# Retention and a Mish feed-forward on one core: the last g sum moved behind the second pair, the sums of w_in for the last tile moved, and one block of the first product moved

## The chip, the cores and the metric

The kernel runs on one core of a Trainium2 chip. The metric is the time of one execution on the device in microseconds (us); the median of several executions counts. A second number beside it is the span, from the first to the last instruction of the program in a profiled execution.

## The reference

```
scores = (q @ k.T) / sqrt(64)                  # q, k, v: 8 batches, 8 heads, 576 rows, 64
ret    = (scores * gamma[h]**(i - j), 0 above the diagonal) @ v
x      = ret, heads side by side               # 4608 tokens x 512
h      = x @ w_in                              # 512 x 2048
g      = h * tanh(softplus(h))                 # Mish
out    = g @ w_out                             # 2048 x 512, float32
```

## The kernel before

**Tiles.** The 4608 tokens are cut into 36 chunks of 128, and four chunks make a tile: nine tiles, t = 0 to 8. While the first product (x @ w_in) of tile t runs, the second product (g @ w_out) of tile t-1 runs between its pieces, and the retention of the next tile's chunks as well, all of it on the same engines. The order on each engine is the order in which the code issues the instructions.

**The second product** uses seven products of half-size matrices in place of eight. Each of the seven is done in two halves, `unit(t-1, k)` for k = 0 to 13, called U0 to U13 below, in the order of products 4, 2, 1, 3, 6, 5, 7 (`ORDER`). Product 7 is thus U12 and U13. One U is eight matmuls at L659. Five of the seven need a sum of two quarters of g; `g_sum(t-1, m)`, called Sm below, makes it on VectorE (L650) in one of three buffers `room`. S7 is read by product 7 alone. When a product is complete, `taken` brings its bank to SBUF on ScalarE (L682, L684, L690, L697, L709) or adds it in on VectorE (L699, L712). L712 takes product 7 and so frees the bank `ops` for product 4 (U0) of the next tile.

**The first product.** `g1(t, f)`, called g4 to g15, makes one block of 128 columns of h: four matmuls (L571) into a bank `hp` of a pool of two, then Mish on ScalarE (L587). The first four columns of blocks in a tile are made by two pairs (A0 with B0, A1 with B1) with seven products in place of eight. `pair_begin` (A) does four small products (L810) into the banks `across` and `along`, ScalarE copies (L830, L831), and GpSimd adds (L832, L833). `pair_end` (B) does three small products more, VectorE combines (L844 reads `across`, L846 reads `along`), and ScalarE applies Mish (L845, L848). The sums of x that the pairs need come from `x_sums` (job X, L805), five on VectorE.

**The last tile** (t = 8, `last` and `tail`) does all its first product by pairs, seven of them. For them it needs sums of quarters of w_in over five more column blocks: `w_in_sum(m)` (L783), five on VectorE, made during t = 7.

**The order around the change.** `PLAN` is written out by hand: sixteen slots for a tile, each a list of jobs, used for t = 3 to 7. In a slot the S and X jobs are issued first, then what belongs to the retention, then the other jobs in order. From t = 3 to 6, slots 4, 5, 12 and 13 each end with the scaling of q and k of one chunk (`step_p`, two instructions at L352 on VectorE); later SyncE transposes it (L374). In slots 6 and 14 a retention visit (L386, L504 and others on TensorE, the mask L392 on VectorE, the copies L516 or L561 on ScalarE) stands ahead of the jobs; for some chunks (`WHOLE`) the slot's jobs are taken in reverse, U12 ahead of g14. GpSimd issues the loads of later chunks (L335, L339); each waits for the latest Mish of a `g1` issued before its slot (`load_ahead`, `so_far`).

The slot's loop, in short:

```
    for t in range(NS, nT - 1):
        for i in range(nF):
            ...
            if t == nT - 2 and i in W_IN:
                w_in_sum(W_IN[i])
            ...
            if t == nT - 2 and i == 15:
                rest()
                x_sums(nT - 1)
            ...
            for job in PLAN[i] ...:   # S and X jobs
            ...                       # retention
            for job in ...:           # A, B, g, U jobs
            ...                       # scaling of a chunk, loads
```

Of the kernel before, what the change touches and what calls it, by code (L numbers as in the profile page):

```python
# [16 lines left out]
def kernel(  # L17
# [40 lines left out]
    nT = n_chunks // NCH  # L58
# [415 lines left out]
    def run(jobs, *how):  # L474
        while jobs:
            jobs.pop()(*how)
# [41 lines left out]
    def visit(n, banks, copies, masked=True):  # L518


        units = states(n + 2)
        for unit in units[:1]:
            unit()
        both = [pool.tile([P, NP, 2, 64], F32, name=name) for pool, name in banks]
        outputs(n, both)
        seen = written(outputs_end(n, both, 0))
        if units:
            step_s(n + 2)
        for unit in units[1:]:
            unit()  # L530
        outputs_end(n, both, 1, seen)
        outputs_copy(n, both, copies)
        if units and masked:
            step_m(n + 2)
# [108 lines left out]
    def g_sum(t, i, engine=nc.vector, to=None):  # L643
        a, b, op_ = {1: ((0, 0), (1, 1), OP.add), 2: ((1, 0), (1, 1), OP.add), 5: ((0, 0), (0, 1), OP.add),
                     6: ((1, 0), (0, 0), OP.subtract), 7: ((1, 1), (0, 1), OP.subtract)}[i]
        if to is None:
            to = room[3 + gsum.setdefault("n", 1) % 3]
            gsum["n"] += 1
        to = to.rearrange("p (f i) -> p f i", f=hF)
        engine.tensor_tensor(to, g_half(t, *a), g_half(t, *b), op=op_)  # L650
        gsum[i] = to
# [18 lines left out]
    def rest():  # L670
        while behind_visit:
            behind_visit.pop(0)()
# [93 lines left out]
    def w_in_quarter(i, j, lo=0, hi=nS):  # L766
        return w_in_t[:, ds(hK * j, hK), :].rearrange("p c (b i q) -> p c b i q", i=2, q=P)[:, :, lo:hi, i, :]

    def w_in_sum_first(i):

        a, b, op_ = W7[i]
        to = {1: kept[:, 0], 5: kept[:, 1], 6: kept[:, 2]}.get(i)
        if to is None:
            to = w_in_quarter(*{2: (1, 0), 7: (0, 1)}[i])
        nc.vector.tensor_tensor(to, w_in_quarter(*a), w_in_quarter(*b), op=op_)
        w7[i, 0] = to

    def w_in_sum(i):

        a, b, op_ = W7[i]  # L780
        to = io.tile([P, 2, H, D], F32, name="qkraw").rearrange("p i h d -> p (i h d)").bitcast(BF16)
        w7[i, 1] = to[:, 0:hK * (nB - nS) * P].rearrange("p (c b q) -> p c b q", c=hK, q=P)
        nc.vector.tensor_tensor(w7[i, 1], w_in_quarter(*a, nS, nB), w_in_quarter(*b, nS, nB), op=op_)  # L783
# [9 lines left out]
    def x_sums(t):  # L793

        if not x_room:
            x_room.append(first.tile([P, 2, H, D], BF16, name="k0", bufs=2).rearrange("p x h d -> p (x h d)"))
            x_room.append(first.tile([P, 2, NP, 64], F32, name="s0", bufs=4)
                          .rearrange("p x n d -> p (x n d)").bitcast(BF16))
            x_room.append(consts.tile([P, hK * hT], BF16, name="xsum"))
        x = lambda j, k: xts[t][:, ds(hK * j, hK), ds(hT * k, hT)]  # L800
        for m, (i, a, b, op_) in enumerate(((3, (0, 1), (1, 1), OP.subtract), (4, (1, 0), (0, 0), OP.subtract),
                                            (6, (0, 0), (0, 1), OP.add), (1, (0, 0), (1, 1), OP.add),
                                            (7, (1, 0), (1, 1), OP.add))):
            x7[i] = x_room[m // 2][:, ts(m % 2, hK * hT)].rearrange("p (c k) -> p c k", c=hK)
            nc.vector.tensor_tensor(x7[i], x(*a), x(*b), op=op_)  # L805
        x7[5], x7[2] = x(1, 1), x(0, 0)
# [274 lines left out]
    for u in range(2, 24):  # L1081
# [43 lines left out]


    PLAN = [x.split() for x in (
        "X S2 g4 g5 U0|S1 U1|A0 U2|g6 U3 B0|g7 U4|U5|g8 U6|S6 g9|U7 g10|S5 U8 g11|U9|S7 A1|g12 U10 B1|g13 U11|g14 U12|g15 U13").split("|")]
    PACED = (1, 2, 3, 4, 5, 6)
    HALVED = {}  # L1130
    WHOLE = (16, 20, 22, 26, 28, 32)
# [14 lines left out]
                load_part(n, part)  # L1146

    LOADS = (2, 3, 4, 5, 6, 7, 8, 9, 11, 12, 13, 14)
    W_IN = {6: 1, 7: 2, 8: 6, 10: 5, 11: 7}
    W_IN_FIRST = {7: 1, 8: 5, 9: 6, 10: 2, 11: 7}  # L1150
    for t in range(NS, nT - 1):
        for i in range(nF):
            n, w = NCH * (t + 1) + i // 8 * 2, i % 8
            copies_first = i == 8 and n - 2 in WHOLE
            if w == (2 if t == NS else 0) and not copies_first:
                run(casts, act)
            if t == nT - 2 and i in W_IN:
                w_in_sum(W_IN[i])
            if t == NS and i in W_IN_FIRST:
                w_in_sum_first(W_IN_FIRST[i])  # L1160
            if t == nT - 2 and i == 15:
                rest()
                x_sums(nT - 1)
            if (t, i) in HALVED:
                halved[0] = HALVED[t, i]
            for job in PLAN[i] if t > NS else {5: ("S5",), 9: ("S7",)}.get(i, ()):
                if job[0] == "S":
                    g_sum(t - 1, int(job[1]))
                elif job == "X":
                    x_sums(t)  # L1170
            if t == NS:
                if w == 6:
                    visit(n, ((ps_h, "hp"), (ps_h, "hp")), (act, act))
            elif n in WHOLE:
                if w == 6:
                    visit(n, ((ps_h, "hp"), (ps_h, "hp")), (act, act))
                elif w == 7:
                    run(sums)
            elif w == 2 and n < n_chunks:
                visit_first(n)  # L1180
            elif w == 6 and n < n_chunks:
                visit_second(n, act)
            if w == (3 if t > NS else 7 if n + 2 == NPE else 0) or w == 0 and n + 2 == NPE:
                run(sums)
            if w in (0, 1) and n + 2 < NPE:
                att(n + 2 + w, "P")
            if w == 1 and n + 4 == NPE:
                more_loads(n + 7)
            ahead = (2, 4) if n + 2 == NPE else (3, 5)
            if t == NS and w in ahead and n + 4 >= NPE:  # L1190
                att(n + 4 + ahead.index(w), "P")
            if t == NS and i == 11:
                behind_visit.pop(0)()
            if t == NS and i == 13:
                rest()
            if w == 0 and n + 2 == NPE:
                tick(t)
            if w == 7 and n + 4 == NPE:
                att(n + 5, "T")
            if w == (4 if n <= NPE - 2 else 7) and n + 4 >= NPE:  # L1200
                att(n + 4, "T")
            if t == NS and n + 2 >= NPE and w in PACED:
                m, part = ((0, 2), (1, 2), (0, 0), (0, 1), (1, 0), (1, 1))[PACED.index(w)]
                tick(t)
                load_part(n + 6 + m, part)
            if w == 5 and n + 4 < NPE:
                more_loads(n + w + 2)
            if w in (4, 5) and n + 2 < NPE:
                att(n - 2 + w, "T")
            if w == (5 if n + 2 == NPE else 7) and n + 2 >= NPE:  # L1210
                att(n + 5, "T")

            if t == NS:
                if i == 14:
                    for s in (2, 3):
                        send(t - 1, s)
                if w == 6:
                    unit(t - 1, BESIDE[i])
                g1(t, i)
                if i in BESIDE and w != 6:  # L1220
                    unit(t - 1, BESIDE[i])
            else:
                if i == 15:
                    rest()
                so_far = done.get(t)
                jobs = PLAN[i]
                for job in reversed(jobs) if n in WHOLE and w == 6 else jobs:
                    if job[0] == "A":
                        pair_begin(int(job[1]))
                    elif job[0] == "B":  # L1230
                        pair_end(t, int(job[1]))
                    elif job[0] == "g":
                        g1(t, int(job[1:]))
                    elif job[0] == "U":
                        unit(t - 1, int(job[1:]))
                        run(crossed)
                        if copies_first:
                            run(casts, act)
                if w in (4, 5):
                    att(n + w, "P")  # L1240
                load_ahead(t, i, so_far)
                if i == 8:
                    rest()
# [32 lines left out]
```

## Time and profile before

| what | value |
|---|---|
| median of 3 runs | 285.26 us (284.73 to 285.44) |
| profiled execution, its own time | 285.38 us |
| its span | 283.7 us |
| mean granted TensorE clock | 0.997 |
| TensorE (PE) busy | 274.6 us, 97% of the span |
| VectorE (DVE) busy | 224.8 us, 79% |
| ScalarE (ACT) busy | 166.1 us, 59% |
| GpSimd (POOL) busy | 143.6 us, 51% |

The profiled execution's own time is 1.7 us over its span and 0.12 us over the median of the runs. A row of the timeline gives the start in us, the duration in us, engine, line and operation, what is written and read, how many instructions are merged in the row, and in brackets the idle time of the engine ahead of it and what ended it. A row of the groups gives busy us, mean ns of one, and the idle time ahead of them. PEld is TensorE's loading of weights, which overlaps the matmuls.

### The profile page before, as it was taken

Reading aid. Unit: us, or ns where it says so; the run is one execution under the profiler, and the core shown is the slowest. Engines: PE = TensorE matmul, PEld = TensorE weight load, DVE = VectorE, ACT = ScalarE, POOL = GpSimd, SP = SyncE. Lnnn points to the kernel's source line nnn. Section 1 sums busy time; section 2 is a strip of 40 time slices with the busy share of each in tenths; the row PEclk is TensorE's granted clock in tenths of the full one; section 3 lists DMA queues with packets and bytes.
Section 4 is the critical chain, followed back from the end, with each engine's and each line's share of the span. In section 5 each row is a group of like instructions: output and inputs, shape, how many; then the busy total and the mean of one; then the engine's idle time right before and its main releaser. Section 6 shows DMA issues by size and latency. Waiting matters only on the chain. (4 is left out here: it accounts for less than half of the span.)

```text
span 283.7 us, 9350 instructions
## 1 busy us (share of the span) xinstructions
PE 274.6 (97%) x4008; PEld 206.4 (73%) x4036; DVE 224.8 (79%) x350; ACT 166.1 (59%) x303; POOL 143.6 (51%) x177
## 2 busy tenths in 40 slices
PE   8999999999999999999999999999999999999994
PEld 3567889988765677767776766777767766888783
DVE  4864779989979959886979886778897695777783
ACT  5656666645776566665666565656566655566620
POOL 8848495875683544453466264627122003559400
PEclk9999999999999999999999999999999999999998
DMA  7999999999999979999999999899955002100333
GB/s 153 155 202 189 193 222 165 194 188 257 172 187 137 213 217 169 179 158 73 240 180 158 92 228 186 188 82 220 101 135 123 5 0 77 74 2 0 113 94 92
DMA packets 77161, 41.24 MB, mean 145 GB/s; under 512 B 60736, under 2 KB 69184, under 8 KB 77120
## 3 DMA queue, kind: packets, MB, share of 16 engines
q0 software_dynamic: 49872, 25.44, 65.2%
q1 hardware_dynamic: 26656, 14.69, 28.6%
q8 instruction: 31, 0.51, 0.9%
q10 hardware_dynamic: 592, 0.52, 0.6%
q14 instruction: 10, 0.08, 0.1%
HBM read 36.70 MB, written 9.44 MB: 163 GB/s over the span
## 5 line engine op out<-in xcount | busy, mean ns | idle before, releaser
L571 PE MATMUL hp<-xT,w_in_t 128*128 128x512 bf16 x314 | 82.8, 379 | 1.9 <-ACT gT L845 0.6
L659 PEld LDWEIGHTS <-room 128*128 128x128 bf16 x656 | 63.3, 98 | 16.3 <-issue 0.7
L587 ACT ACTIVATE gT<-hp 128x512 bf16<-128x512 f32 x93 | 55.5, 598 | 33.4 <-PE hp L571 30.7
L650 DVE TENSOR_TENSOR room<-gT 128x2048 bf16<-128x2048 bf16 x43 | 52.7, 1244 | 1.1 <-ACT gT L587 1.1
L571 PEld LDWEIGHTS <-w_in_t 128*128 128x128 bf16 x344 | 33.3, 98 | 26.8 <-issue 1.1
L832 POOL TENSOR_TENSOR k<-k 128x256 f32<-128x256 f32 x10 | 10.6, 1062 | 64.5 <-ACT k L830 64.5
L659 PE MATMUL ops<-room,room 128*128 128x256 bf16 x336 | 42.3, 273 | 0.2 <-ACT res L697 0.2
L352 DVE TENSOR_TENSOR qks<-qkraw,gqk 128x512 bf16<-128x512 f32 x56 | 35.2, 684 | 0.7 <-DMA qkraw<-in_k_dram 0.7
L659 PEld LDWEIGHTS <-gT 128*128 128x128 bf16 x288 | 27.5, 98 | 6.8 <-issue 0.6
L659 PE MATMUL ops<-w_out_t,room 128*128 128x256 bf16 x224 | 28.7, 273 | 0.1
L335 POOL DMA_DIRECT2D qkraw<-in_q_dram x24 | 21.8, 908 | 11.4 <-DMA vs<-in_v_dram 6.6
L335 POOL DMA_DIRECT2D qkraw<-in_k_dram x24 | 21.6, 899 | 10.5 <-ACT gT L587 10.3
L335 POOL DMA_DIRECT2D vs<-in_v_dram x24 | 21.6, 902 | 10.3 <-ACT gT L587 10.3
L844 DVE TENSOR_TENSOR k<-k,hp 128x512 f32<-128x512 f32 x10 | 6.9, 686 | 17.7 <-PE hp L810 12.8
L392 DVE TENSOR_TENSOR sm<-sc,mask 128x1024 bf16<-128x1024 f32 x14 | 17.1, 1220 | 4.0 <-PE sc L386 4.0
L598 PE MATMUL hp<-xT,w_in_t 128*128 128x128 bf16 (+1 forms) x184 | 15.3, 240 | 0.0
L456 DVE TENSOR_TENSOR total<-sc,total 128x256 f32<-128x256 f32 x32 | 13.5, 423 | 0.8
L659 PE MATMUL ops<-room,gT 128*128 128x256 bf16 x112 | 13.7, 273 | 0.4 <-DVE res L712 0.2
L598 PEld LDWEIGHTS <-w_in_t 128*128 128x128 bf16 x184 | 13.1, 98 | 1.1 <-DVE xT L255 0.2
L845 ACT ACTIVATE gT<-hp 128x512 bf16<-128x512 f32 x10 | 6.0, 597 | 12.9 <-DVE k L844 12.9
L516 ACT CAST xT<-hp 128x512 bf16<-128x512 f32 x18 | 9.7, 589 | 6.6 <-PE hp L504 6.5
L601 ACT ACTIVATE gT<-hp 128x512 bf16<-128x512 f32 x16 | 9.6, 600 | 5.4 <-PE hp L598 5.4
(201 smaller groups left out, 509.7 us busy)
## 6 DMA issues: line engine op xcount, KB each, us to landing
out_dram<-res SPq DMA_DIRECT2D x29, 256.0 KB, 4.8
qkraw<-in_q_dram POOLq DMA_DIRECT2D x24, 256.0 KB, 5.6
qkraw<-in_k_dram POOLq DMA_DIRECT2D x24, 256.0 KB, 6.0
vs<-in_v_dram POOLq DMA_DIRECT2D x24, 128.0 KB, 5.1
w_out_t<-in_moe_w_out_dram POOLq DMA_DIRECT2D x4, 512.0 KB, 11.6
w_in_t<-in_moe_w_in_dram POOLq DMA_DIRECT2D x6, 256.0 KB, 8.1
out_dram<-res SPq DMA_DIRECT2D x9, 128.0 KB, 2.5
qkraw<-in_q_dram POOLq DMA_DIRECT2D x8, 128.0 KB, 5.9
```

Of the source, the lines that this page charges most:

```text
L335: ins = nc.gpsimd.dma_start(out=t, in_=src[b, :, ds(P * c, P), :].rearrange("h p d -> p h d"))
L352: nc.vector.tensor_tensor(slots[:, :, y], heads[:, :, y], factors[:, :, y].unsqueeze(3).to_broadcast([P, NP, 2, D]), op=OP.mult)
L392: nc.vector.tensor_tensor(sm.rearrange("p e x n i -> p (e x n) i"), live[n]["sc"].rearrange("p e x n i -> p (e x n) i"), mask.unsqueeze(1) ...
L456: nc.vector.tensor_tensor(new[:, k], st[:, j, x], total[b], op=OP.add)
L516: copy(xts[t][:, :, ds(P * s, 2 * P)].rearrange("p h (x j i) -> p j h x i", x=2, j=2)[:, j], both[j])
L571: nc.tensor.matmul(to, lhsT=w, rhs=x, start=first, stop=last)
L587: done[t] = nc.scalar.activation(gts[t][:, f, :], hp, AX.Mish)
L598: nc.tensor.matmul(hp[:, a].rearrange("p (e k) -> p e k", e=2)[:, e], lhsT=w_in_t[:, c, ts(2 * i + a, P)], rhs=x1[j][:, e, c, :], start=(a ...
L601: nc.scalar.activation(gts[1][:, ds(2 * i, 2), ds(2 * P * j, 2 * P)], hp, AX.Mish)
L650: engine.tensor_tensor(to, g_half(t, *a), g_half(t, *b), op=op_)
L659: nc.tensor.matmul(bank[:, half, :], lhsT=g[:, f, ts(half, P)], rhs=w[:, f, :], start=(f == 0 and half == 0 and not add), stop=(f == hF - ...
L832: nc.gpsimd.tensor_tensor(z[:, 0], z[:, 0], z[:, 1], op=OP.add)
```

## The change

Three edits in the written order, none in what is computed.

S7 moves from the head of slot 11 (ahead of A1) to the head of slot 13 (behind B1). g11 moves from slot 9, behind U8, to slot 8, behind g10 and ahead of U8. Both hold for t = 3 to 7.

The five sums of w_in, in t = 7 alone, stood in slots 6, 7, 8, 10 and 11. Now two stand in slot 4, two in slot 5, and the fifth in slot 15. Their place in the slot changes too: they come behind `x_sums` of the last tile, where that is issued (slot 15).

```
-        "X S2 g4 g5 U0|S1 U1|A0 U2|g6 U3 B0|g7 U4|U5|g8 U6|S6 g9|U7 g10|S5 U8 g11|U9|S7 A1|g12 U10 B1|g13 U11|g14 U12|g15 U13").split("|")]
+        "X S2 g4 g5 U0|S1 U1|A0 U2|g6 U3 B0|g7 U4|U5|g8 U6|S6 g9|U7 g10 g11|S5 U8|U9|A1|g12 U10 B1|S7 g13 U11|g14 U12|g15 U13").split("|")]
...
-    W_IN = {6: 1, 7: 2, 8: 6, 10: 5, 11: 7}
+    W_IN = {4: (1, 2), 5: (6, 5), 15: (7,)}
...
-            if t == nT - 2 and i in W_IN:
-                w_in_sum(W_IN[i])
             if t == NS and i in W_IN_FIRST:
                 w_in_sum_first(W_IN_FIRST[i])
             if t == nT - 2 and i == 15:
                 rest()
                 x_sums(nT - 1)
+            for m in W_IN.get(i, ()) if t == nT - 2 else ():
+                w_in_sum(m)
```

## The prediction

> **What bounds the kernel now.** I read the page first, then the groups by line and the list of waits, then the timeline of each tile's eighth to fifteenth slot. Tiles are numbered by t as in the loops; the five that follow PLAN are t = 3 to 7.
>
> ```profile
> PE 274.6 (97%) x4008; PEld 206.4 (73%) x4036; DVE 224.8 (79%) x350; ACT 166.1 (59%) x303; POOL 143.6 (51%) x177
> L571 PE MATMUL hp<-xT,w_in_t 128*128 128x512 bf16 x314 | 82.8, 379 | 1.9 <-ACT gT L845 0.6
> L659 PE MATMUL ops<-room,room 128*128 128x256 bf16 x336 | 42.3, 273 | 0.2 <-ACT res L697 0.2
> PEld L386 <- issue: 1.3, 4, 0.6
> ```
>
> TensorE is busy 97% of the span, and the idle time before its two great groups of products is 1.9 and 0.2 us. So there are hardly any waits that a change could remove, while every wait added on TensorE lengthens the run by its own size. VectorE at 79% has gaps, but its order is fixed: what stands behind a moved sum comes later. The question is thus where each moved sum ends, against the moment at which TensorE wants it.
>
> **Sum 7 behind the second pair.** One tile in full, t = 4, from the timeline (start, us, engine, line):
>
> ```profile
> 146.34 1.22 DVE L650 TENSOR_TENSOR room<-gT 128x2048 bf16<-128x2048 bf16 x1
> 147.18 0.96 POOL L832 TENSOR_TENSOR k<-k 128x256 f32<-128x256 f32 x1 [1.46 <-ACT k L830]
> 148.21 0.72 POOL L833 TENSOR_TENSOR k<-k,one 128x256 f32<-128x256 f32 x1
> 148.30 0.38 PE L810 MATMUL hp<-xT,w_in_t 128*128 128x256 bf16 x2
> 148.97 0.69 DVE L844 TENSOR_TENSOR k<-k,hp 128x512 f32<-128x512 f32 x1 [1.42 <-POOL k L833]
> 149.76 0.69 DVE L846 TENSOR_TENSOR k<-st,k 128x512 f32<-128x512 f32 x1
> 150.37 2.49 DVE L352 TENSOR_TENSOR qks<-qkraw,gqk 128x512 bf16<-128x512 f32 x4
> 151.88 1.05 PE L659 MATMUL ops<-room,room 128*128 128x256 bf16 x8
> ```
>
> The first row is sum 7 (S7): VectorE does it at 146.34, then sits idle for 1.42 us until GpSimd's second add (L833) lets it subtract (L844). S7 lies in a gap and costs nothing. The last row is U12, the first half of product 7, at 151.88: the reader of S7.
>
> After the change VectorE's order is L844, L846, two of the four L352 (the scaling of q and k of one chunk), S7, the other two L352. From L844 to the place of the third L352 is 2.60 us: 0.79 to L846, 0.61 to L352, and 1.20 for two of the four (half of 2.49, less 0.045: neighbours overlap a little). S7 adds 1.22, and the product starts 0.05 behind its operand (so in the last fence, L712 and the product after it). U12 can start 3.87 us after L844 starts.
>
> When does L844 start then? S7 no longer lies beside GpSimd's add, which these rows of t = 7 show undisturbed:
>
> ```profile
> 218.21 0.72 POOL L832 TENSOR_TENSOR k<-k 128x256 f32<-128x256 f32 x1 [10.54 <-ACT k L830]
> 220.49 0.38 PE L810 MATMUL hp<-xT,w_in_t 128*128 128x256 bf16 x2
> 220.98 0.69 DVE L844 TENSOR_TENSOR k<-k,hp 128x512 f32<-128x512 f32 x1 [2.83 <-PE hp L810]
> ```
>
> Alone L832 takes 0.72, against 0.96 beside S7. So in t = 4 GpSimd is done at 147.18 + 0.72 + 0.08 + 0.72 = 148.70. But L844 also reads the bank `across`, whose last product ends at 148.30 + 0.38 = 148.68, and L844 follows such an end by 0.11 (220.98 against 220.87). It starts at 148.79, 0.18 earlier than now and no more: TensorE's own order holds it. U12 starts at 148.79 + 3.87 = 152.66 in place of 151.88: TensorE stands 0.78 us. The same for the other tiles that have L352 behind the pair, two rows each, with GpSimd's first add:
>
> ```profile
> 119.29 1.24 POOL L832 TENSOR_TENSOR k<-k 128x256 f32<-128x256 f32 x1 [1.94 <-ACT k L830]
> 120.69 0.38 PE L810 MATMUL hp<-xT,w_in_t 128*128 128x256 bf16 x2
> 124.34 0.93 PE L659 MATMUL ops<-room,room 128*128 128x256 bf16 x7
> ...
> 176.51 1.24 POOL L832 TENSOR_TENSOR k<-k 128x256 f32<-128x256 f32 x1 [2.38 <-ACT k L830]
> 177.92 0.38 PE L810 MATMUL hp<-xT,w_in_t 128*128 128x256 bf16 x2
> 181.37 1.05 PE L659 MATMUL ops<-room,room 128*128 128x256 bf16 x8
> ...
> 205.63 1.24 POOL L832 TENSOR_TENSOR k<-k 128x256 f32<-128x256 f32 x1 [4.94 <-ACT k L830]
> 207.03 0.38 PE L810 MATMUL hp<-xT,w_in_t 128*128 128x256 bf16 x2
> 210.71 1.04 PE L659 MATMUL ops<-room,room 128*128 128x256 bf16 x8
> ```
>
> GpSimd's two adds would end 1.52 after L832's start: 120.81, 178.03 and 207.15, each before the bank's end (121.07, 178.30, 207.41). So the bank decides: L844 at 121.18, 178.41, 207.52, U12 at 125.05, 182.28, 211.39, late by 0.71, 0.91 and 0.68. Sum over t = 3 to 6: 0.71 + 0.78 + 0.91 + 0.68 = 3.1 us.
>
> What is queued behind S7 on VectorE: the second chunk's scaling, its transposes on SyncE, the mask (L392), the state sums, L710 and L712, and the next tile's X, S2 and S1. All come 0.95 later (1.13 that S7 takes of the queue, less the 0.18), but TensorE has by then stood 0.7 to 0.9, so against it they slip by at most 0.25. L712, which frees the bank of the next U0, has that much room by the order of t = 4. I take nothing for it; up to 0.1 per tile, 0.4, is its bound.
>
> **The moved block of the first product.** g11 goes ahead of U8 with nothing added. It needs a hp bank that g9 gave up one U and one g before, so it doesn't wait. U8 comes one block later, which takes away the wait behind the copy at L697: 0.2 at the most by the second group above, I take 0.1.
>
> **Sums of w_in (L783) and the last PLAN tile.** In t = 7 no chunk is scaled any more.
>
> ```profile
> 224.70 1.22 DVE L392 TENSOR_TENSOR sm<-sc,mask 128x1024 bf16<-128x1024 f32 x1 [1.50 <-PE sc L386]
> ...
> 233.51 0.82 DVE L783 TENSOR_TENSOR qkraw<-w_in_t 128x1280 bf16<-128x1280 bf16 x1
> 233.70 2.34 POOL L832 TENSOR_TENSOR k<-k 128x256 f32<-128x256 f32 x1 [13.97 <-ACT k L830]
> 235.11 0.38 PE L810 MATMUL hp<-xT,w_in_t 128*128 128x256 bf16 x2
> 236.41 1.04 PE L659 MATMUL ops<-w_out_t,room 128*128 128x256 bf16 x8
> 237.46 0.23 PE L504 MATMUL sc<-qkT,last 64*64 64x64 bf16 x8
> 237.60 0.60 ACT L845 ACTIVATE gT<-hp 128x512 bf16<-128x512 f32 x1 [2.78 <-DVE k L844]
> 238.25 1.02 PE L571 MATMUL hp<-xT,w_in_t 128*128 128x512 bf16 x4 [0.55 <-ACT gT L845]
> 238.57 0.59 ACT L709 COPY dmask<-ops 128x512 f32<-128x512 f32 x1
> 239.57 1.08 ACT L561 CAST xT<-sc 128x512 bf16<-128x512 f32 x2
> 240.68 0.76 DVE L805 TENSOR_TENSOR k<-xT 128x512 bf16<-128x512 bf16 x2 [0.80 <-ACT xT L561]
> 242.37 0.68 DVE L712 TENSOR_TENSOR res<-res,ops 128x512 f32<-128x512 f32 x1
> 243.10 1.03 PE L659 MATMUL ops<-room,gT 128*128 128x256 bf16 x8 [0.24 <-DVE res L712]
> ```
>
> Four sums go to slots 4 and 5, ahead of L392, where one stands now: three more, at 0.74 each (0.82 less the overlap) 2.2 us, against 1.50 of idleness. L392 slips by some 0.7; sum 6 of g behind it does not, since the w_in sum that stood between them is gone. The masked scores of L392 are wanted only in slot 10, so this costs nothing; that cover is full, though, and a fifth sum there would push sum 6.
>
> In slot 11 a w_in sum and S7 both leave GpSimd's add (2.34 us there, 0.72 alone). L844 then starts by the bank, 235.49 + 0.11 = 235.60, L845 0.72 later at 236.32, not 237.60, and g14 no longer waits 0.55 for it. S7 follows L846 at once, ends 2.62 after 235.60, at 238.22, and U12 comes at 238.5: no wait here.
>
> But the fifth sum now stands between X and L712. ScalarE takes L709 when U11 ends (237.45 + 0.08), L561 1.00 later as now, and ends 1.08 after that: X at 239.64, 1.04 earlier than 240.68. X's five sums take 1.69 of the queue, the w_in sum 0.74 (0.82 less the overlap), so L712 starts at 242.07 against 242.37 and U0, which waits for it, comes 0.30 earlier. Most of what slot 11 gives is handed back at slot 15. From there TensorE sets the pace again.
>
> **The sum.** 3.1 - 0.1 - 0.3 = +2.7 us on the profiled execution's 285.38, 288.1. That execution is 0.12 above the median of the runs shown, so 288.0 for the median. One unknown: inside L386 TensorE's weight loads once stand 0.6 us on "issue", with no semaphore behind it. Changed timing may remove this or bring another: 0.7 each way.
>
> **A rule against this.** GpSimd issues loads in slots 12 and 13, where S7 now lies. Here S5 of t = 3 lay beside such an issue:
>
> ```profile
> 115.84 1.22 DVE L650 TENSOR_TENSOR room<-gT 128x2048 bf16<-128x2048 bf16 x1
> 116.47 0.88 POOL L335 DMA_DIRECT2D vs<-in_v_dram  x1 [1.68 <-ACT gT L587]
> ```
>
> Neither was longer than usual. The Trainium skill, SBUF — State Buffer, section "SBUF: two separate sides", says that VectorE and GpSimd hold a shared port pair by an exclusive lock, and that a GpSimd DMA's descriptors can't be written while VectorE holds it. The slowed L832 agrees with the lock; the pair of rows above doesn't show it for an issue.
>
> **The rivals.** (1) Other side, faster: S7 is done before U12 wants it, and t = 7's relief carries through. It decides where L844 starts 3.87 us ahead of U12, so 0.7 to 0.9 us earlier than the bank's end allows in t = 3 to 6. Then the 0.55 and 0.24 shown as waits in t = 7 and some 0.3 of semaphore lag around them go: 285.26 - 1.1 = 284.2. For it speaks only that VectorE idles before L844 (1.42); against, that this idleness ends with TensorE's own product. Chance 0.05. (2) S7 is hidden, but the fifth w_in sum gives back slot 11's relief: 285.26 - 0.4 = 284.9, within the noise. Chance 0.05. (3) S7 and the GpSimd issues exclude each other, and S7 waits for one issue of 0.88 in each of four tiles: 288.0 + 3.5 = 291.5. The two rows speak against it. Chance 0.04. (4) The change as worked out: 0.86.
>
> **How the numbers follow.** The likeliest case gives 288.0. Its own range: 0.7 for the issue stall, 0.1 per tile either way on four waits, 0.3 on t = 7, which reaches from 286.9 to 289.1 when the larger ones add up. To hold 8 in 10 with the rivals on both sides I go to 286.4 and 289.3. About 0.3% (0.86 us) is what a measurement of this kernel can tell from no change: slower than 286.1 takes cases (3) and (4), 0.90; faster 0.05; the same 0.05.
>
> **What would show it.** Right: in t = 3 to 6 VectorE's L650 stands between two pairs of L352, and U12 has 0.7 to 0.9 us of idle time ended by L650; L832 takes 0.72 in slot 11 everywhere; in t = 7 g14 doesn't wait for L845, an L783 stands before the L712 there, and U0's wait for it grows. Wrong: no idle time of TensorE ahead of U12, which would mean that L844 started far earlier; or L650 itself lengthened beside L335, which is case (3); or idle time at the next tile's U0, which would put the bound of 0.4 on top.

## The result, and the profile after

The change makes the kernel slower: 287.70 us median against 285.69, 23 executions of each side by side; ratio 1.0084, 95% interval 1.0059 to 1.0108, which is +2.4 us (1.7 to 3.1). The forecast was +2.7. The ratio leaves out disturbed, slow executions (two of the kernel before took 471 and 721 us, for example), so it is not the quotient of the two medians, which lie 2.0 us apart.

The changed kernel was profiled a second time, as the first of the experiments below, because the first profiled execution (294.14 us) held a stall of over 3 us at L386, with the granted clock (the share of full speed that TensorE is given) at half behind it. The second has neither; the last section has the figures. All rows of "after" are from the second. First the page and the groups (busy us, mean ns, idle time ahead and what ended it), then two lines of its list of waits (us in total, times, longest):

```profile
PE 274.9 (96%) x4008; PEld 205.8 (72%) x4036; DVE 224.5 (78%) x350; ACT 166.0 (58%) x303; POOL 139.9 (49%) x177
L659 PE MATMUL ops<-room,room 128*128 128x256 bf16 x336 | 42.0, 273 | 2.9 <-DVE room L650 2.9
L832 POOL TENSOR_TENSOR k<-k 128x256 f32<-128x256 f32 x10 | 7.2, 721 | 67.1 <-ACT k L830 67.1
PE ops L659 <- DVE room L650: 2.9, 4, 0.9
PE ops L659 <- DVE res L712: 0.7, 1, 0.7
```

The idle time ahead of TensorE's largest group of the second product went from 0.2 to 2.9 us, in four waits, all ended by L650, the g sums. GpSimd's first add now takes 0.72 us in all ten places. That relief is real, and it buys little.

The four waits in the timeline, for t = 3 with VectorE's rows ahead of the wait:

```profile
122.13 0.38 PE L810 MATMUL hp<-xT,w_in_t 128*128 128x256 bf16 x2
122.62 0.69 DVE L844 TENSOR_TENSOR k<-k,hp 128x512 f32<-128x512 f32 x1 [1.58 <-PE hp L810]
123.41 0.69 DVE L846 TENSOR_TENSOR k<-st,k 128x512 f32<-128x512 f32 x1
124.02 1.28 DVE L352 TENSOR_TENSOR qks<-qkraw,gqk 128x512 bf16<-128x512 f32 x2
124.85 0.91 POOL L335 DMA_DIRECT2D qkraw<-in_k_dram  x1
124.91 1.04 PE L571 MATMUL hp<-xT,w_in_t 128*128 128x512 bf16 x3
125.22 1.22 DVE L650 TENSOR_TENSOR room<-gT 128x2048 bf16<-128x2048 bf16 x1
126.36 1.29 DVE L352 TENSOR_TENSOR qks<-qkraw,gqk 128x512 bf16<-128x512 f32 x2
126.50 1.05 PE L659 MATMUL ops<-room,room 128*128 128x256 bf16 x8 [0.56 <-DVE room L650]
...
152.74 0.32 PE L432 MATMUL sc<-vs,qks 64*64 64x64 bf16 x16
154.84 1.05 PE L659 MATMUL ops<-room,room 128*128 128x256 bf16 x8 [0.83 <-DVE room L650]
...
182.11 0.32 PE L432 MATMUL sc<-vs,qks 64*64 64x64 bf16 x16
184.21 1.05 PE L659 MATMUL ops<-room,room 128*128 128x256 bf16 x8 [0.95 <-DVE room L650]
...
212.65 1.04 PE L571 MATMUL hp<-xT,w_in_t 128*128 128x512 bf16 x3
214.24 1.05 PE L659 MATMUL ops<-room,room 128*128 128x256 bf16 x8 [0.55 <-DVE room L650]
```

S7 (L650 at 125.22) stands between two pairs of L352, as the new order says, 2.60 us behind L844, and U12 (126.50) follows 3.88 behind L844. The idle time in brackets is counted from the modelled end of the matmul before, so for the time lost I take the distance from the start of the stretch ahead (g14 in t = 3 and 6, the visit's first L432 in t = 4 and 5) to U12, against the same distance in the kernel before, whose rows are these:

```profile
123.47 1.04 PE L571 MATMUL hp<-xT,w_in_t 128*128 128x512 bf16 x3
150.57 0.32 PE L432 MATMUL sc<-vs,qks 64*64 64x64 bf16 x16
180.18 0.32 PE L432 MATMUL sc<-vs,qks 64*64 64x64 bf16 x16
209.83 1.04 PE L571 MATMUL hp<-xT,w_in_t 128*128 128x512 bf16 x3
```

With U12 at 124.34, 151.88, 181.37 and 210.71 there: 1.59 - 0.87, 2.10 - 1.31, 2.10 - 1.19 and 1.59 - 0.88, that is 0.72, 0.79, 0.91 and 0.71, in sum 3.13 us.

The last PLAN tile, t = 7, after:

```profile
237.24 0.72 POOL L832 TENSOR_TENSOR k<-k 128x256 f32<-128x256 f32 x1 [13.97 <-ACT k L830]
238.65 0.38 PE L810 MATMUL hp<-xT,w_in_t 128*128 128x256 bf16 x2
239.14 0.69 DVE L844 TENSOR_TENSOR k<-k,hp 128x512 f32<-128x512 f32 x1 [2.37 <-PE hp L810]
241.17 1.04 PE L571 MATMUL hp<-xT,w_in_t 128*128 128x512 bf16 x4
243.19 0.76 DVE L805 TENSOR_TENSOR k<-xT 128x512 bf16<-128x512 bf16 x2 [0.80 <-ACT xT L561]
244.87 0.82 DVE L783 TENSOR_TENSOR qkraw<-w_in_t 128x1280 bf16<-128x1280 bf16 x1
245.61 0.68 DVE L712 TENSOR_TENSOR res<-res,ops 128x512 f32<-128x512 f32 x1
246.34 1.03 PE L659 MATMUL ops<-room,gT 128*128 128x256 bf16 x8 [0.65 <-DVE res L712]
```

g14 (241.17) carries no wait any more. But the fifth w_in sum stands between X and L712, and U0 waits 0.65 by the row, where it waited 0.24. From the bank's last product to U0 it is 246.34 - 238.65 = 7.69 us, before 243.10 - 235.11 = 7.99: the tile gains 0.30.

### The profile page after: what moved, and what is told of

It is laid out like the page before. It is cut to its first block, busy times and chain, and to the rows that moved or that the text cites. A ratio compares the mean times of both kernels' runs of the same rounds, so it can differ in the third digit from the quotient of the medians.

```text
span 292.4 us, 9352 instructions
## 1 busy us (share of the span) xinstructions
PE 277.6 (95%) x4008; PEld 207.0 (71%) x4036; DVE 225.4 (77%) x350; ACT 166.0 (57%) x303; POOL 140.1 (48%) x177
## 5 line engine op out<-in xcount | busy, mean ns | idle before, releaser
L587 ACT ACTIVATE gT<-hp 128x512 bf16<-128x512 f32 x93 | 55.0, 597 | 36.7 <-PE hp L571 33.6
L571 PEld LDWEIGHTS <-w_in_t 128*128 128x128 bf16 x344 | 33.7, 99 | 28.2 <-issue 2.2
L650 DVE TENSOR_TENSOR room<-gT 128x2048 bf16<-128x2048 bf16 x43 | 52.6, 1243 | 1.1 <-ACT gT L587 1.1
L832 POOL TENSOR_TENSOR k<-k 128x256 f32<-128x256 f32 x10 | 7.4, 742 | 67.1 <-ACT k L830 67.1
L352 DVE TENSOR_TENSOR qks<-qkraw,gqk 128x512 bf16<-128x512 f32 x56 | 35.6, 686 | 2.1 <-DMA qkraw<-in_k_dram 2.1
L844 DVE TENSOR_TENSOR k<-k,hp 128x512 f32<-128x512 f32 x10 | 6.9, 688 | 21.8 <-PE hp L810 21.8
L598 PEld LDWEIGHTS <-w_in_t 128*128 128x128 bf16 x184 | 13.1, 98 | 1.1 <-DVE xT L255 0.2
L601 ACT ACTIVATE gT<-hp 128x512 bf16<-128x512 f32 x16 | 9.6, 600 | 5.4 <-PE hp L598 5.4
L810 PEld LDWEIGHTS <-w_in_t 128*128 128x128 bf16 x116 | 11.3, 98 | 1.3
```

The costliest lines, as they stand in the source:

```text
L352: nc.vector.tensor_tensor(slots[:, :, y], heads[:, :, y], factors[:, :, y].unsqueeze(3).to_broadcast([P, NP, 2, D]), op=OP.mult)
L571: nc.tensor.matmul(to, lhsT=w, rhs=x, start=first, stop=last)
L587: done[t] = nc.scalar.activation(gts[t][:, f, :], hp, AX.Mish)
L598: nc.tensor.matmul(hp[:, a].rearrange("p (e k) -> p e k", e=2)[:, e], lhsT=w_in_t[:, c, ts(2 * i + a, P)], rhs=x1[j][:, e, c, :], start=(a ...
L601: nc.scalar.activation(gts[1][:, ds(2 * i, 2), ds(2 * P * j, 2 * P)], hp, AX.Mish)
L810: nc.tensor.matmul(to, lhsT=w7_of(i, b, c), rhs=x7[i][:, c, :], start=(start and c == 0), stop=(c == hK - 1), skip_group_check=True)
```

## The experiments

The theory under test: U12 waits for S7, because two L352 stand ahead of S7, and the fifth w_in sum hands back what t = 7 gains. The rivals: other parts of the change cost the time, or what is queued behind S7 does. Seven kernels came first, then a series of three. The expected times stand on the median shown before the change, 285.26; the kernel before was run again beside the experiments, with medians of 285.6 to 286.0, and each ratio below is to those runs.

**The changed kernel itself.**

> The changed kernel itself, for a profile beside the runs of the kernel before. Theory (U12 waits for the moved sum 7): idle time of TensorE ahead of U12 of about 0.7, 0.8, 0.9 and 0.7 us in t = 3 to 6, ended by L650; none in t = 7; U0 of the last tile waits 0.8 for L712. 287.5 to 288. Rival (late transposes: the second chunk is scaled 1.1 later, so its transposed rows land late and the scores at L386 wait): waits of a us or more inside L386 in every tile.

Measured: 287.69 us, ratio 1.0058 (1.0019 to 1.0098), which is +1.7. The rows above are its own. U12's waits and U0's are there; its list of waits has no DMA that ended a wait at L386. So the rival of late transposes doesn't hold for this execution. The first profiled execution has one such wait, of 0.6 us, just ahead of its long stall; the rival asks for one of a us or more in every tile.

**Sum 7 alone.** PLAN with S7 moved; g11 and the w_in sums as before.

```
-  |S7 A1|g12 U10 B1|g13 U11|
+  |A1|g12 U10 B1|S7 g13 U11|
```

> Only sum 7 is moved, the w_in sums and g11 are as before. Theory: U12's four waits stay (+3.1). In t = 7 sum 7 no longer lies beside GpSimd's add, L844 starts about 1.1 earlier (one w_in sum still lies there), g14's wait of 0.74 goes, and since the fifth w_in sum does not stand ahead of L712, U0's wait goes too: -1.1. Sum +2.0: 287.3. Rival (g11 or the w_in sums cost the time): no more than +0.3, 285.6.

Measured: 288.17 us, ratio 1.0066 (1.0030 to 1.0101), scattered from 286.83 to 289.55. The time is 0.9 above the one expected, but against the kernel before beside it the ratio gives +1.9, where +2.0 was expected. So the move of S7 by itself makes the kernel slower, and the other parts aren't needed for it. The profiled execution (289.55) had a stall inside L386 as well, to which the last section comes back. t = 7 went as expected:

```profile
238.69 0.81 DVE L783 TENSOR_TENSOR qkraw<-w_in_t 128x1280 bf16<-128x1280 bf16 x1
238.89 1.21 POOL L832 TENSOR_TENSOR k<-k 128x256 f32<-128x256 f32 x1 [13.97 <-ACT k L830]
240.93 0.69 DVE L844 TENSOR_TENSOR k<-k,hp 128x512 f32<-128x512 f32 x1 [1.42 <-PE st L810]
246.52 0.68 DVE L712 TENSOR_TENSOR res<-res,ops 128x512 f32<-128x512 f32 x1
247.25 1.03 PE L659 MATMUL ops<-room,gT 128*128 128x256 bf16 x8
```

With one w_in sum still beside it, GpSimd's add takes 1.21 instead of 2.34, and L712 comes in time: U0 has no wait in brackets. From the bank's last product (240.29) to U0 it is 6.96 us, where the kernel before took 7.99.

**Sum 7 back in slot 11**, the rest of the change kept.

```
-  |U9|A1|g12 U10 B1|S7 g13 U11|
+  |U9|S7 A1|g12 U10 B1|g13 U11|
```

> The changed kernel with sum 7 back at the head of slot 11. Theory: no wait ahead of U12; L844 of t = 7 still starts some 1.1 earlier than in the kernel before, and the fifth w_in sum at slot 15 hands most of it back: -0.4 against before, 284.9. Rival (g11 or the w_in sums cost the time): 287 or more.

Measured: 284.63 us, ratio 0.9963 (0.9925 to 1.0001). On the same chip as the changed kernel it is 3.06 us below it; the sum for S7 was 3.1. That the two agree to less than 0.1 is luck, since each median is uncertain by about 1 us (the ratio's interval reaches 0.4% either way). The rival is out all the same: it asked for 287 or more. In t = 3:

```profile
119.38 1.24 POOL L832 TENSOR_TENSOR k<-k 128x256 f32<-128x256 f32 x1 [1.45 <-ACT k L830]
121.45 0.69 DVE L844 TENSOR_TENSOR k<-k,hp 128x512 f32<-128x512 f32 x1 [0.63 <-POOL k L833]
124.43 1.04 PE L659 MATMUL ops<-room,room 128*128 128x256 bf16 x8
```

The slowed add is back, L844 waits for GpSimd again, and none of it matters: U12 has no wait.

**Sum 7 ahead of the scaling.** S7 right behind L846.

```
-  |S7 g13 U11|
+  |g13 U11|
 ...
+                if i == 12:
+                    g_sum(t - 1, 7)
                 if w in (4, 5):
                     att(n + w, "P")
```

> The changed kernel with sum 7 issued right behind L846, ahead of the first chunk's scaling (L352) instead of behind it. Theory (it is the 1.20 us of two L352 that make sum 7 late): sum 7 ends 2.6 after L844 starts, 0.2 to 0.5 before U12 wants it in each tile; no wait; 284.9. Rival (what is queued behind sum 7 is late: second chunk, its transposes, mask, L712): all of that stays as late as in the changed kernel, so 287.5.

Measured: 285.73 us, ratio 0.9995 (0.9961 to 1.0028): 2.0 below the changed kernel, but 0.8 above what I expected. Two stretches of its timeline, t = 3, and the end of t = 4:

```profile
123.39 1.22 DVE L650 TENSOR_TENSOR room<-gT 128x2048 bf16<-128x2048 bf16 x1
124.53 2.49 DVE L352 TENSOR_TENSOR qks<-qkraw,gqk 128x512 bf16<-128x512 f32 x4
125.15 1.04 PE L659 MATMUL ops<-room,room 128*128 128x256 bf16 x8
...
157.97 0.68 DVE L712 TENSOR_TENSOR res<-res,ops 128x512 f32<-128x512 f32 x1
158.70 1.47 PE L659 MATMUL ops<-room,gT 128*128 128x256 bf16 x12 [0.63 <-DVE res L712]
```

U12's wait is gone, as the theory has it: so it is the two L352 that make S7 late. But the rival holds too, in one place above all: everything behind S7 is still about a us late, and at the turn from t = 4 to 5 the late L712 holds up U0, 0.63 us by the row. Counted between the bank's last products, from the second pair of a tile to the first pair of the next, the turns behind t = 3, 4 and 5 took 0.12, 0.69 and 0.22 longer than in the kernel with S7 back (for t = 4 from 149.23 to 165.06, against 148.39 to 163.53), 1.0 of the 1.1 us between the two medians. In the changed kernel the late L712 doesn't show, since TensorE has stood as long ahead of U12.

**Sum 7 one slot later**, behind both chunks' scaling.

```
-  |S7 g13 U11|g14 U12|
+  |g13 U11|S7 g14 U12|
```

> The changed kernel with sum 7 one slot later still, at the head of slot 14, behind the scaling of both chunks. Theory: in t = 3 to 6 two more L352 (1.20) stand ahead of it and U12 waits 1.20 longer in each: +4.8 on the changed kernel, 292.4; in t = 7, where nothing is scaled, no difference. Rival (the time goes to the chunk's lateness and not to U12): the second chunk is on time again here, so this is faster than the changed kernel, about 286.

Measured: 293.87 us, ratio 1.0299 (1.0259 to 1.0340). The profiled execution took 292.29. In t = 3, and in the list of waits:

```profile
125.21 1.22 DVE L650 TENSOR_TENSOR room<-gT 128x2048 bf16<-128x2048 bf16 x1
126.49 1.05 PE L659 MATMUL ops<-room,room 128*128 128x256 bf16 x8 [1.76 <-DVE room L650]
PE ops L659 <- DVE room L650: 7.7, 4, 2.2
```

Four waits grew from 2.9 to 7.7 us: 4.8 for eight more L352 (0.6 each), though the second chunk is scaled on time. The lateness of the chunk isn't what costs; U12's wait follows the dose. The six executions lost more than this: their median is 6.2 us above the changed kernel's, on another chip, where 4.8 was expected. The profiled one was the fastest of them; what the others lost beyond the four waits is open.

**The fifth w_in sum in slot 14** instead of 15.

```
-    W_IN = {4: (1, 2), 5: (6, 5), 15: (7,)}
+    W_IN = {4: (1, 2), 5: (6, 5), 14: (7,)}
```

> The changed kernel with the fifth w_in sum in slot 14 in place of slot 15, so ahead of the five sums of x instead of between them and L712. Theory: VectorE is idle there until ScalarE's casts of x come (L561), so the sum costs nothing, L712 starts 0.74 earlier and U0's wait of 0.8 goes: -0.8 on the changed kernel, 286.8. Rival (U0's wait is set by something else, such as the end of U13): no difference.

Measured: 287.66 us, ratio 1.0067 (1.0035 to 1.0100): no difference in time that the scatter would let me see, where 0.8 was expected. The trace does show the wait go:

```profile
240.84 0.82 DVE L783 TENSOR_TENSOR qkraw<-w_in_t 128x1280 bf16<-128x1280 bf16 x1
244.04 0.68 DVE L712 TENSOR_TENSOR res<-res,ops 128x512 f32<-128x512 f32 x1
244.78 1.03 PE L659 MATMUL ops<-room,gT 128*128 128x256 bf16 x8
```

**Both repairs.** S7 in slot 11 and the fifth sum in slot 14.

> Both repairs: sum 7 back in slot 11 and the fifth w_in sum in slot 14; what is left of the change is the w_in sums out of GpSimd's way and g11. Theory: no wait ahead of U12, g14's wait of t = 7 gone and U0's wait gone: 0.74 + 0.10 + 0.41 less about 0.15 because sum 7 still lies beside GpSimd's add in t = 7: -1.1 on the kernel before, 284.2. Rival (the relief in t = 7 is eaten later in the last tile): no faster than the kernel before.

Measured: 284.46 us, ratio 0.9967 (0.9939 to 0.9995). It is faster than the kernel before by little, and the next series has it so again.

**A dose of w_in sums ahead of L712.** S7 is in slot 11 in all three. None (the kernel just told, once more), one (the kernel with S7 back, once more), or two sums stand between X and L712:

```
 none:  W_IN = {4: (1, 2), 5: (6, 5), 14: (7,)}
 one:   W_IN = {4: (1, 2), 5: (6, 5), 15: (7,)}
 two:   W_IN = {4: (1, 2), 5: (6,), 15: (5, 7)}
```

> Sum 7 of g in slot 11 in all three of this call, so no wait ahead of U12; the kernels differ in how many w_in sums stand between X and L712 in slot 15 of t = 7. Here none (the fifth is in slot 14). Theory (VectorE's queue ahead of L712 sets when U0 of the last tile starts): no wait of U0 for L712 beyond 0.1; 284.2. Rival (the scatter between executions covers all of this): no order among the three.

> One w_in sum between X and L712, as in the changed kernel. Theory: U0 waits 0.8 longer than with none, shown as 0.65 behind L712 in the trace; 0.8 above the kernel with none, 285.0. Rival: no order among the three.

> Two w_in sums between X and L712 (one more is moved there from slot 5). Theory: 0.74 more again (0.82 less the overlap), U0 shown as waiting 1.4 behind L712; 285.7. Rival: no order among the three.

Measured: 284.53, 285.06 and 285.18 us; ratios 0.9950 (0.9918 to 0.9982), 0.9963 (0.9926 to 1.0000), 0.9983 (0.9955 to 1.0011). In order, but the intervals overlap, and the steps of 0.5 and 0.1 are smaller than the 0.8 and 0.74 expected. The list of waits gives the dose cleanly: with none it has no such line, with one the first, with two the second:

```profile
PE ops L659 <- DVE res L712: 0.7, 1, 0.7
PE ops L659 <- DVE res L712: 1.4, 1, 1.4
```

The medians show no more than the order; the traces settle the size. From the bank's last product in t = 7 to U0 it is 6.96 us with none (234.45 to 241.41), 7.69 with one (234.42 to 242.11) and 8.42 with two (237.09 to 245.51): 0.73 for each sum. And from the L712 ahead of this U0 to the end of the span, all twelve profiles of this document take 41.3 to 41.4 us, whatever came before. What is lost ahead of that U0 is thus lost at the end of the execution.

## Why the prediction was right

**TensorE sets the time.** As read: at 97% busy, each wait added there came out in the end. The changed kernel's new idle time stands in two places, ahead of U12 and ahead of U0.

**L844's start.** I said that the bank `across` and not GpSimd would hold it, 0.11 behind the bank's last product. In t = 3 that product ends at 122.13 + 0.38 = 122.51, and L844 starts at 122.62. The relief of the add was thus worth 0.2 us of VectorE's time and nothing to TensorE in t = 3 to 6, which the kernel with S7 back confirms from the other side.

**U12.** 3.87 behind L844 was forecast, 3.88 measured. The four waits, 0.71, 0.78, 0.91 and 0.68, came out as 0.72, 0.79, 0.91 and 0.71: 3.13 us for 3.1. The move of S7 alone, taken back, gave 3.06 in whole executions.

**t = 7.** 0.30 was forecast and 0.30 measured, by the same two terms: g14's wait went, and the fifth sum took most of it.

**g11.** It wasn't tried by itself, but the traces show what it gave. In the kernel with S7 alone, where g11 stands as before, U8 of t = 5 still waits for L697, the same wait as in the kernel before:

```profile
PE ops L659 <- ACT res L697: 0.2, 1, 0.2
```

The changed kernel's list has no such line. From the bank's last product of the first pair of t = 5 to that of the second, the kernel with S7 alone takes 13.75 us (167.74 to 181.49), the changed one 13.44 (166.40 to 179.84). So g11 gave 0.31, where the forecast took 0.1 and called 0.2 the most: it went by the idle time in the list, which is counted from a modelled end and here shows about half of what was lost.

**What was queued behind S7.** The step that said L712 "has that much room by the order of t = 4", at most 0.1 per tile, held, but only under the cover of U12's wait. With that wait taken away and the queue left late, U0 stood 0.63 us. The working compared VectorE's delay with TensorE's, which was right; for the kernel with S7 ahead of the scaling I forgot it, and expected 0.8 too little.

**The lock.** The rival that S7 and GpSimd's load issues exclude each other is out: in t = 3 the issue at 124.85 took 0.91 and S7 beside it 1.22, neither longer than alone; in t = 4 and 5, where S7 lay beside issues as well, it took 1.22 too. The Trainium skill, SBUF — State Buffer, section "SBUF: two separate sides", gives VectorE's part in the lock to an instruction "in a 2-port perf mode, or with two SBUF inputs (only against a GpSimd op that reads SBUF)", and has a DMA's descriptors held up while VectorE runs one in a 2-port mode. For GpSimd's adds the traces agree (0.72 alone, 1.24 beside one sum, 2.34 beside two). For its load issues beside S7, a sum of two SBUF inputs, no run here shows a lock.

**The size.** The forecast of +2.7 was 0.3 above the measured +2.4, well inside its interval of 1.7 to 3.1. With g11 as measured, the traces give 3.13 - 0.31 - 0.30 = 2.5; the term for g11 was the one that was too small. The two profiled executions are further apart, 3.24 us at the U0 behind t = 7 (246.34 against 243.10). The second was 1.44 behind at the first pair of t = 3 already (the bank's last product at 107.20 against 105.76), ahead of everything that the change moves, and the first lost 0.73 in t = 5 to a stall inside L386 (14.48 us from the first pair to the second, against 13.75 with S7 alone): 1.44 + 2.52 - 0.73 = 3.23. That the forecast time of 288.0 lies so near 287.70 is partly luck: it stands on a median of three executions, 285.26, where 23 gave 285.69.

## What to carry to other kernels

Before moving a job later on an engine that works in order, compare two moments: when its reader wants it, and when the new place in the queue ends; the jobs it is moved behind count in full. A gap on an engine that is not the bound is the cheapest place for a job, even where the job slows a neighbour there, so long as that neighbour's own reader waits for something later. A wait that is removed can be taken up by the next queue, as with the sum that stood ahead of L712: follow what is issued between the removed wait and the next thing that TensorE needs.

## What the runs showed of the hardware

TensorE now and then stands in the middle of the 64 x 64 products of L386. The lists of waits have this in five of the twelve profiles, with 0.3 to 2.7 us for one stall; for the kernel before the list has 0.5, and the distance between starts gives 0.7. Two lines, from the kernel with S7 alone and from the one with two sums ahead of L712:

```profile
PE sc L386 <- issue: 1.5, 1, 1.5
PE sc L386 <- DMA qkT<-qks: 1.1, 1, 1.1
```

The second names the transposed rows' landing; the first, like most of the others, names no semaphore. These stalls come in some executions of either kernel and not in others, and lengthen those that have them; the kernel before scattered from 284.5 to 289.9 us beside the series of three. What they are was not tried and stays open.

Once such a stall cost about twice its length. In the first profiled execution of the changed kernel, TensorE stood 0.56 and then 2.68 us in one burst of L386, between 110.2 and 113.9 us. The granted clock was 0.50 from 113 to 116 us and 0.54 from 116 to 120, and 1.00 from 106 to 110 and from 120 to 124. From the first pair of t = 3 to the second (L844 at 106.90 and 128.12) this execution took 6.3 us longer than the second one (107.69 and 122.62). This is one case; behind the shorter stalls of the other profiles the mean granted clock of the execution stayed at 0.997 or more.
